# Where 64 rows of the gate and up weights land in SBUF: partitions 32 to 95 in place of 0 to 63 and 64 to 127

## The chip, the core and the metric

The kernel runs on one core of a Trainium2 chip. A core has a matrix engine (PE, whose loading of stationary operands is listed apart as PEld), three engines for elementwise work (DVE, ACT, POOL), a queue engine that issues DMAs (SP), 16 DMA engines between the chip's memory (HBM) and the on-chip memory SBUF, and PSUM, into which PE writes. SBUF has 128 partitions; a tile is a block of partitions by columns. Each engine takes its instructions in the order in which they were written for it, and waits on semaphores for what others produce. The metric is the device time of one execution in microseconds.

## The reference

Forward and backward pass of a small decode block, in bfloat16: a layer norm of `x` (2 rows of 576), attention of 32 query heads over a cache of 16 heads of 4096 positions by 128, and beside it a gated bilinear layer with 4608 columns. Its outputs are the result and the gradients of `x`, both caches and all five weight matrices.

```python
xn = _layernorm(x, axis=-1)
out = x + A(xn, k_cache, v_cache, wq, wo) + B(xn, w_gate, w_up, w_down)

def B(x, w_gate, w_up, w_down):
    g = x @ w_gate          # [2, 576] @ [576, 4608]
    u = x @ w_up
    return (g * u) @ w_down
out, vjp = jax.vjp(f, x, k_cache, v_cache, wq, wo, w_gate, w_up, w_down)
grads = vjp(grad_out)
```

The caches are read once and their gradients written once, in blocks of 1 MB: 92.5 MB in and 92.5 MB out in all, weights included.

## The kernel before

All of it is one program with streams of work: loads of the caches (`load_kv`), loads of weights (`load_ws`), 32-by-32 transposes of what was loaded (`turn`, on DVE), softmax (`attend`), its gradient (`dscores`), the outer products that make the cache gradients (`outer`), the projections per group of heads (`group_front`, `group_back`) and the gated layer in nine slices of 512 columns (`mlp`). A planner (`class Order`) runs through these streams before anything is built, with an estimate for each operation and hand-tuned priorities (`PR`, `OFF`), and so fixes the order on every engine. What it decides is fixed in the program; at run time each engine waits only on semaphores. All large DMAs are issued by SP, in one order; an issue waits until the eighth before it has landed.

The gated layer's weights have 576 rows. Rows 0 to 511 of a pair of slices go to a `big` tile, four rows to each of 128 partitions, in rows of 2 KB (1 KB for the last slice, which is alone). Rows 512 to 575, the rest, go to the tile `gu` (L1158): those of the gate matrix to partitions 0 to 63, those of the up matrix to partitions 64 to 127, in the same columns. There are five pairs of these loads, four of 128 KB and one of 64 KB each. The loads of the rest of `wq` (rows 512 to 575, 512-byte rows, two halves of the columns on the two halves of the partitions, L1132) are made in the same manner and are not touched by the change.

Three steps use `gu`:

- In the forward product (`mlp`, L854) the fifth of five accumulating matmuls takes `gu` as moving operand, with a stationary `xs[:, 4]` (the normed `x` on partitions 0 to 63, zero elsewhere) for the gate and `xs[:, 5]` (on partitions 64 to 127) for up. `front` fills both from two small transposes on PE.
- For the gradient of `x`, `mlp` transposes the weights on DVE: the main part into `X`, `gu` into `Xt` (256 columns of 4 bytes, one instruction for gate and up).
- `dxn` (L678 and L683) multiplies these with stationaries: `wm` for the main part and `wt` for the rest. `stationaries` makes `wm` on DVE (L664) and then two halves of `wt` from it on POOL (L671), one for the partitions of gate and one for those of up. The product has 128 columns for the main part and 32 for the rest, and is added to `accx` (160 columns, L944). The query weights use the same function, with `accx` too (L1085). `final_dx` folds `accx` into the gradient with small float32 matmuls (L1486, L1488).

The softmax steps use small tiles (`mx`, `m4`, `mr`, `negb`, `z`, `rz`, `cs`, `cr`), two sets of them, and constants are made through short-lived tiles (`S64`, `mk16`, `foldf`, `xnb`), each with memory of its own.

Of the kernel before, what the change touches and what calls it, by code (L numbers as in the profile page):

```python
# [250 lines left out]
def DVE(cost):  # L251
    return ("op", "DVE", cost)
# [6 lines left out]
def POOL(cost):  # L259
    return ("op", "POOL", cost)  # L260
# [10 lines left out]
def REL(tag, i):  # L271
    return ("rel", tag, i)
# [24 lines left out]
NBIG, NGU, NWW, NBD = 16, 1, 6, 3  # L297
# [56 lines left out]
def kernel(  # L354
# [31 lines left out]
    GH = 2 * G  # L386
# [8 lines left out]
    FS = 512  # L395
# [11 lines left out]
    def tiles(tag, n, shape, dtype=BF16):  # L407
        od.ring(tag, n)
        return [const.tile(list(shape), dtype, name=f"{tag}{i}") for i in range(n)]

    kv_t = X_t = st_t = G_t = tiles("big", NBIG, [P, NCH * Dh])
    od.share("big", CAP)
    Xt_t = tiles("Xt", 1, [P, FS])
    gu_t = tiles("gu", NGU, [P, 2 * FS])
    ww_t = tiles("ww", NWW, [P, WB])
    tl_t = tiles("tl", 2, [P, FS])
    BD_t = tiles("BD", NBD, [P, 16, Dh])
# [21 lines left out]
    ch_t = []  # L439
    for i in range(2):  # L440
        ch_t.append(dict(
            mx=const.tile([P, 1], FP32, name=f"mx{i}"), m4=const.tile([1, 4], FP32, name=f"m4{i}"),
            mr=const.tile([1, P], FP32, name=f"mr{i}"),
            negb=const.tile([P, 1], FP32, name=f"negb{i}"), ex=const.tile([P, P], FP32, name=f"ex{i}"),
            z=const.tile([P, 1], FP32, name=f"z{i}"), rz=const.tile([P, 1], FP32, name=f"rz{i}"),
            pr=const.tile([P, P], BF16, name=f"pr{i}"), cs=const.tile([P, 1], FP32, name=f"cs{i}"),
            cr=const.tile([P, 1], FP32, name=f"cr{i}"), ds=const.tile([P, P], BF16, name=f"ds{i}"),
            sp=const.tile([P, 2 * P], BF16, name=f"sp{i}")))

# [5 lines left out]
    m_t = banks("m", 2, [P, 512])  # L455
# [4 lines left out]
    def pairs(ap):  # L460
        return ap.bitcast(FP32)

    def t32(out, in_):
        nc.vector.transpose(out, in_)  # L464
# [30 lines left out]
    acc = filled("acc", [P, 5, 2], FP32, 0.0)  # L495
    accx = filled("accx", [P, 160], FP32, 0.0)
    xs = filled("xs", [P, 6, 32], BF16, 0.0)
    Wdy = filled("Wdy", [P, 2, 160], BF16, 0.0)
# [14 lines left out]
    Q4 = const.tile([P, 4], FP32, name="Q4")  # L513
    S64 = const.tile([P, 64], FP32, name="S64")
    G4 = const.tile([P, 32, 4], FP32, name="G4")
    mask8 = const.tile([P, 4, 2], FP32, name="mask8")
    mk16 = const.tile([P, 2, 8], FP32, name="mk16")
    mask16 = const.tile([P, 16], BF16, name="mask16")
    fold = const.tile([P, 4, GH], BF16, name="fold")
    foldf = const.tile([P, 4, GH], FP32, name="foldf")  # L520

# [71 lines left out]
    def front():  # L593
# [31 lines left out]
        nc.vector.tensor_copy(xs[64:128, 5, 0:2], tp[64:128, 10:12])  # L625
        yield REL("m", i)
        yield SET(Exn)
# [33 lines left out]
    def stationaries(i, rep, npos, half, costs):  # L661
        Wm, Wt = wm_t[i], wt_t[i]
        yield DVE(costs[0])
        nc.vector.tensor_tensor(  # L664
            view(Wm[:], 0, P, 0, [[8, npos], [2, 4], [1, 2]]), view(rep, 0, P, 0, [[2, npos], [0, 4], [1, 2]]),
            view(mask8[:], 0, P, 0, [[0, npos], [2, 4], [1, 2]]), ALU.mult)
        yield POOL(costs[1])
        for h in range(2):
            off, dims = half(h)
            n = len(dims) > 1 and dims[0][1] or 1  # L670
            nc.gpsimd.tensor_copy(  # L671
                view(Wt[:], 64 * h, 64, 0, [[dims[-1][1], n], [1, dims[-1][1]]]), view(Wm[:], 64 * h, 64, off, dims))

    def dxn(dp, i, X, S, pos, xoff, xstep, Xt, St, toff, tpos):
        Wm, Wt = wm_t[i], wt_t[i]
        for s in range(S):
            for q in range(4):
                nc.tensor.matmul(dp[32 * q:32 * q + 32, 0:P], lhsT=view(Wm[:], 0, P, 8 * pos(q, s), [[1, 32]]),  # L678
                                 rhs=view(X, 0, P, xoff(q, s), [[xstep, 4], [2, 32]]),
                                 start=(s == 0), stop=(s == S - 1))  # L680
        for s in range(St):
            for q in range(4):
                nc.tensor.matmul(dp[32 * q:32 * q + 32, P:160], lhsT=view(Wt[:], 0, P, 8 * tpos(q, s), [[1, 32]]),  # L683
                                 rhs=view(Xt, 0, P, toff(q, s), [[2, 32]]),
                                 start=(s == 0), stop=(s == St - 1))
# [152 lines left out]
    def mlp(i, hh, sl, Lgu, Ld, wd_slot):  # L838
# [4 lines left out]
        f0 = i * FS  # L843
# [93 lines left out]
        dxn(m_t[m], ws, X[:], 8, lambda q, s: q * 8 + s,  # L937
            lambda q, s: (s // 4) * 4 * FS + (2 * q + (s // 2) % 2) * 64 + s % 2, FS,
            Xt[:], 4, lambda q, s: (2 * q + s // 2) * 64 + s % 2, lambda q, s: 4 * q + s)
# [80 lines left out]
    def group_back(g):  # L1020
# [46 lines left out]
        for be in range(4):  # L1067
# [11 lines left out]
        yield PE(0.24, 0.17, kind="c")  # L1079
        dxn(m_t[m], ws, X[:], 4, lambda q, s: q * 4 + s, lambda q, s: (2 * q + s // 2) * 64 + s % 2, FS,  # L1080
            X[:], 2, lambda q, s: 4 * FS + q * 64 + s, lambda q, s: 2 * q + s)
        yield REL("X", x)
        yield REL("wm", ws)
        yield DVE(0.31)
        nc.vector.tensor_add(accx[:], accx[:], m_t[m][:, 0:160])  # L1085
        yield REL("m", m)
# [36 lines left out]
    def load_w(item):  # L1123
# [20 lines left out]
        else:  # L1144
# [6 lines left out]
            for w, Wsrc in enumerate((B_w_gate, B_w_up)):  # L1151
                b = yield ACQ("G")
                sl["G"].append(b)
                yield DMA("SP", 0.4, 128 * 4 * width * 2, 2 * width)
                nc.sync.dma_start(G_t[b][:, 0:4 * width].rearrange("p (c n) -> p c n", n=width),
                                  Wsrc[0:512, f0:f0 + width].rearrange("(p c) n -> p c n", c=4))
                yield DMA("SP", 0.36, 64 * width * 2, 2 * width)
                nc.sync.dma_start(gu[64 * w:64 * w + 64, 0:width], Wsrc[512:576, f0:f0 + width])  # L1158
            yield ("lset", Lgu)
# [317 lines left out]
    def final_dx():  # L1477
# [7 lines left out]
        yield PE(0.3, 0.3)  # L1485
        nc.tensor.matmul(mt[:, 0:8], lhsT=accx[:, 0:P], rhs=F8[:], start=True, stop=True)  # L1486
        for k in range(2):
            nc.tensor.matmul(mt[0:32, 8:12], lhsT=accx[:, P:160], rhs=F8[:, 4 * k:4 * k + 4],  # L1488
                             start=(k == 0), stop=(k == 1))
        rows_add(o, 1)  # L1490
# [69 lines left out]
```

## Time and profile before

| | |
|---|---|
| device time, three runs | 477.23, 479.78, 479.92 us; median 479.78 |
| profiled execution: span from the first to the last instruction | 475.9 us |
| profiled execution's own time | the page gives none beside the span; the three runs are 1.3 to 4.0 us above it |
| bytes | 92.48 MB read, 92.48 MB written; 389 GB/s over the span |
| mean granted clock of PE | 0.713 |
| DMA packets | 41925 |
| `gu` loads, issue to landing (min / median / max) | 10.1 / 12.6 / 14.6 us |

The profile is of one execution. Its page lists the busy time of each engine, the DMA queues, the chain of work that ended last (followed back from the last instruction to what released it, again and again), and the costliest groups of instructions by line: engine, operation, output and inputs, shapes, count, then busy time in us and the mean of one in ns, then the idle time of the engine ahead of them and what ended it. A table by stretches gives the busy time of each engine between two times, with the DMA share (the mean busy share of the 16 engines) and the rate in GB/s. Busy time of an engine that is not on the chain costs nothing.

### The profile page before, as it was taken

The numbers are of one execution on the slowest core, as the hardware profiler recorded it, in microseconds if no ns is written. First come the engines' busy times: TensorE is split into PE (matmuls) and PEld (weight loads), VectorE is DVE, ScalarE is ACT, GpSimd is POOL, SyncE is SP. The second block draws the span as 40 slices with busy tenths as digits, with TensorE's granted clock in tenths as the row PEclk, the third lists the DMA queues.
The fourth block names the chain that finished last, engine by engine and source line by source line (L and its number), as shares of the span: only waits on it lengthen the run. The fifth ranks groups of instructions, "written<-read, shape, count | busy, mean of one in ns | idle before, by whom it ended". The sixth has DMA issues, their size and how long they took to land.

```text
span 475.9 us, 15396 instructions
## 1 busy us (share of the span) xinstructions
PE 369.1 (78%) x6546; PEld 214.3 (45%) x6546; DVE 369.3 (78%) x708; ACT 335.2 (70%) x507; POOL 152.4 (32%) x208
## 2 busy tenths in 40 slices
PE   1588589879598868678768977797777879878894
PEld 1455344445464535454453444563334424434463
DVE  8897878869658976687758868899577958888771
ACT  3149569958676886536779764599676987898971
POOL 0440154351004443004634510051644656333000
PEclk9979585758756678577767685679665866776965
DMA  8999999999999999999999999999999999999994
GB/s 317 364 401 420 399 410 402 355 392 423 419 400 390 391 356 420 424 407 375 370 407 372 324 412 421 419 412 398 337 425 417 416 416 421 423 420 392 425 354 185
DMA packets 41925, 185.95 MB, mean 391 GB/s; under 512 B 3960, under 2 KB 13440, under 8 KB 25472
## 3 DMA queue, kind: packets, MB, share of 16 engines
q1 hardware_dynamic: 41848, 184.96, 98.4%
q8 instruction: 51, 0.84, 0.7%
q14 instruction: 18, 0.15, 0.1%
q10 hardware_dynamic: 8, 0.00, 0.0%
HBM read 92.48 MB, written 92.48 MB: 389 GB/s over the span
## 4 chain that ended last, share of the span: by engine, by line
DMA 46%; PE 21%; DVE 15%; ACT 10%; issue 4%; POOL 2%; SPq 1%; DVEq 0%; ACTq 0%; POOLq 0%
DMA out_dram<-big 20%; DMA big<-in_A_v_cache_dram 12%; DVE big L464 10%; ACT big L468 8%; DMA big<-in_A_k_cache_dram 8%; PE ps_o L1255 4%; PE ps_m L1234 4%; DMA ww<-in_A_wo_dram 3%; PE ps_o L722 3%; DMA gu<-in_B_w_up_dram 3%; DVE big L470 2%; PE ps_m L1407 2%; POOL BD L1222 2%; PE ps_m L678 1%; PE ps_o L759 1%
## 5 line engine op out<-in xcount | busy, mean ns | idle before, releaser
L468 ACT CAST big<-ps_o 128x1024 bf16<-128x1024 f32 (+2 forms) x310 | 277.4, 960 | 45.7 <-PE ps_o L1255 20.0
L464 DVE STREAM_TRANSPOSE big<-big 128x1024 f32<-128x1024 f32 x146 | 175.9, 1224 | 28.8 <-DMA out_dram<-big 16.8
L1222 POOL TENSOR_TENSOR BD<-vr,mask 128x2048 bf16<-128x2048 bf16 x32 | 115.3, 3604 | 102.6 <-ACT vr L468 48.6
L470 DVE CAST big<-ps_o 128x1024 bf16<-128x1024 f32 (+2 forms) x68 | 74.4, 1095 | 15.8 <-PE ps_o L722 5.2
L1234 PE MATMUL ps_m<-big,W 128*32 128x128 bf16 x2048 | 59.1, 279 | 10.2 <-ACT Q L468 3.4
L1234 PEld LDWEIGHTS <-W 128*32 128x32 bf16 x2048 | 46.1, 123 | 27.1 <-issue 25.2
L671 POOL COPY wt<-wm 64x128 bf16<-64x128 bf16 (+1 forms) x34 | 8.9, 263 | 139.5 <-DVE wm L664 119.3
L1255 PE MATMUL ps_o<-BD,dd 32*128 32x512 bf16 x256 | 45.3, 476 | 10.2 <-ACT big L468 8.0
L1255 PE MATMUL ps_o<-BD,pp 32*128 32x512 bf16 x256 | 47.1, 507 | 6.2 <-ACT big L468 3.5
L1199 POOL COPY W<-rep 32x16 bf16<-32x16 bf16 x128 | 24.9, 194 | 54.1 <-DVE rep L983 32.2
L464 DVE STREAM_TRANSPOSE big<-ww 128x1152 f32<-128x1152 f32 x25 | 34.0, 1361 | 6.9 <-DMA ww<-in_A_wo_dram 3.5
L1407 PE MATMUL ps_m<-big,pp 128*32 128x512 bf16 x256 | 27.9, 507 | 5.0 <-DMA big<-in_A_v_cache_dram 4.3
L1255 PEld LDWEIGHTS <-dd 32*128 32x128 bf16 x256 | 12.2, 98 | 32.3 <-issue 26.9
L1407 PE MATMUL ps_m<-big,dd 128*32 128x512 bf16 x256 | 24.7, 473 | 0.8 <-DVE acc L919 0.6
L1255 PEld LDWEIGHTS <-pp 32*128 32x128 bf16 x256 | 10.4, 96 | 27.1 <-issue 23.6
L759 PEld LDWEIGHTS <-xnr 32*128 32x128 bf16 x368 | 12.9, 114 | 12.3 <-issue 10.9
L722 PE MATMUL ps_o<-dyr,R 32*32 32x288 bf16 x256 | 17.1, 398 | 1.7 <-ACT big L468 1.3
L872 PE MATMUL ps_m<-big,Wdy 128*128 128x128 bf16 x162 | 15.0, 265 | 2.9 <-DVE rz L1320 1.4
L722 PE MATMUL ps_o<-dyr,hb 32*32 32x288 bf16 x288 | 16.2, 346 | 0.4 <-ACT big L468 0.2
L759 PE MATMUL ps_o<-D,xnr 32*128 32x128 bf16 x256 | 13.3, 281 | 3.4 <-ACT big L468 1.5
L872 PEld LDWEIGHTS <-Wdy 128*128 128x128 bf16 x162 | 13.4, 119 | 5.0 <-issue 5.0
L678 PE MATMUL ps_m<-big,wm 128*32 128x128 bf16 x416 | 12.7, 280 | 3.4 <-DVE rz L1320 1.2
(205 smaller groups left out, 478.2 us busy)
## 6 DMA issues: line engine op xcount, KB each, us to landing
out_dram<-big SPq DMA_DIRECT2D x74, 1024.0 KB, 12.6
big<-in_A_k_cache_dram SPq DMA_DIRECT2D x32, 1024.0 KB, 13.8
big<-in_A_v_cache_dram SPq DMA_DIRECT2D x32, 1024.0 KB, 13.5
out_dram<-big SPq DMA_DIRECT2D x17, 576.0 KB, 11.0
ww<-in_B_w_down_dram SPq DMA_DIRECT2D x9, 576.0 KB, 12.8
ww<-in_A_wo_dram SPq DMA_DIRECT2D x8, 576.0 KB, 7.3
ww<-in_A_wq_dram SPq DMA_DIRECT2D x8, 512.0 KB, 8.1
big<-in_B_w_gate_dram SPq DMA_DIRECT2D x4, 1024.0 KB, 11.5
```

Source lines behind the costliest of these rows:

```text
L464: nc.vector.transpose(out, in_)
L468: nc.scalar.copy(out, in_)
L470: nc.vector.tensor_copy(out=out, in_=in_)
L678: nc.tensor.matmul(dp[32 * q:32 * q + 32, 0:P], lhsT=view(Wm[:], 0, P, 8 * pos(q, s), [[1, 32]]), rhs=view(X, 0, P, xoff(q, s), [[xstep, 4 ...
L722: nc.tensor.matmul(o[32 * q:32 * q + 32, aa, 0:HD2], lhsT=view(t, 32 * q, 32, 2 * A + aa, [[4, 32]]), rhs=dyr[32 * q:32 * q + 32, k * HD2: ...
L759: nc.tensor.matmul(o[:, aa, j * P:(j + 1) * P], lhsT=xnr[32 * a:32 * a + 32, dc * P:(dc + 1) * P], rhs=rhs(a), start=True, stop=True)
L872: nc.tensor.matmul(dh, lhsT=Wdy[:, e, 2 * k:2 * k + P], rhs=view(X[:], 0, P, 64 * k + e, [[D, FC], [2, 32]]), start=(k == 0 and e == 0), s ...
L1199: nc.gpsimd.tensor_copy(view(W_t[t][w][:], 32 * a, 32, 6 + 8 * a, [[G * WW, 4], [WW, G], [1, 2]]), view(rep_t[grp[g]["qs"]][:], 32 * a, 32 ...
L1222: nc.gpsimd.tensor_tensor(BD_t[i][:], view(vr_t[v][:], 0, P, 0, [[0, 16], [1, Dh]]), view(mask16[:], 0, P, 0, [[1, 16], [0, Dh]]), ALU.mult)
L1234: nc.tensor.matmul(sc[32 * cq:32 * cq + 32, :], lhsT=view(W[:], 0, P, (be * G + l) * WW + 6 - 4 * c2 - 2 * l, [[1, 32]]), rhs=view(X[:], 0 ...
L1255: nc.tensor.matmul(o[:, k, :], lhsT=pr2[32 * c4:32 * c4 + 32, :], rhs=BD[32 * c4:32 * c4 + 32, 8 * l + 4 * h2:8 * l + 4 * h2 + 4, :], star ...
L1407: nc.tensor.matmul(ct[32 * j:32 * j + 32, :], lhsT=view(rT, 0, P, 4 * c + 2 * l, [[1, 32]]), rhs=kv_t[kvS[s][t][l]][:, Dh * c:Dh * (c + 4) ...
```

## The change

The rest of both matrices now goes to partitions 32 to 95, in columns of their own: gate in the first half of the columns of `gu`, up in the second, so that `gu` is twice as wide. Partitions 0 to 31 and 96 to 127 of it are cleared once, by two instructions on POOL, since PE multiplies all 128 partitions. What follows from it:

- one stationary `xs[:, 6]` (the normed `x` on partitions 32 to 95) in place of two; `front` makes it with one more transpose on PE and two copies on DVE. `xs[:, 4]` and `xs[:, 5]` stay for the query weights;
- `Xt` has twice the columns, and its transpose takes 512 columns of 4 bytes in place of 256;
- in `dxn`, `mlp` uses `wm` itself for the rest, with 32 matmuls in place of 16 for each slice; the two copies to `wt` on POOL are left out for the nine slices (18 instructions). Those for the query weights stay;
- the rest's product of the slices goes to columns 0 to 31 of `accx`, that of the query weights to 160 to 191, so that `accx` has 192 columns and `final_dx` a third small product;
- to make room, the small tiles of a softmax set become columns of one tile `small`, `mr` lies in the tile `sp`, `S64`, `mk16` and `foldf` in `ex` of the first set, and `xnb` in the last `BD` tile.

Apart from what is added and left out, the instructions stand in the same order on every engine, the DMAs on SP's queue too. In the waits, the copy to `sp` waits for ACT in one place more, the first transpose of `gu` also waits for POOL (the clearing), and some of DVE's `wm` products no longer wait for POOL.

```diff
-    Xt_t = tiles("Xt", 1, [P, FS])
-    gu_t = tiles("gu", NGU, [P, 2 * FS])
+    Xt_t = tiles("Xt", 1, [P, 2 * FS])
+    gu_t = tiles("gu", NGU, [P, 4 * FS])
...
+        small = const.tile([P, 12], FP32, name=f"small{i}")
         ch_t.append(dict(
...
+            {k: small[:, j:j + 1] for j, k in enumerate(("mx", "negb", "z", "rz", "cs", "cr"))}, m4=small[0:1, 8:12],
+            ex=const.tile([P, P], FP32, name=f"ex{i}"), pr=const.tile([P, P], BF16, name=f"pr{i}"),
+            ds=const.tile([P, P], BF16, name=f"ds{i}"), sp=const.tile([P, 2 * P], BF16, name=f"sp{i}")))
+        ch_t[i]["mr"] = ch_t[i]["sp"][0:1].bitcast(FP32)
...
-    accx = filled("accx", [P, 160], FP32, 0.0)
-    xs = filled("xs", [P, 6, 32], BF16, 0.0)
+    accx = filled("accx", [P, 192], FP32, 0.0)
+    xs = filled("xs", [P, 7, 32], BF16, 0.0)
+    for t in gu_t:
+        for r in (slice(0, 32), slice(96, P)):
+            nc.gpsimd.memset(t[r], 0.0)
...
-    S64 = const.tile([P, 64], FP32, name="S64")
+    S64 = ch_t[0]["ex"][:, 0:64]
...
-    xnb = const.tile([2, D], BF16, name="xnb")
+    xnb = BD_t[NBD - 1][0:2].rearrange("p a d -> p (a d)")[:, 0:D]
...
+        nc.tensor.transpose(tp[0:96, 12:14], xnb[:, 480:576], ident[0:2, 0:2])
...
+        for r in (slice(32, 64), slice(64, 96)):
+            nc.vector.tensor_copy(xs[r, 6, 0:2], tp[r, 12:14])
...
         yield POOL(costs[1])
+        if half is None:
+            return
...
-                t, c0 = (main[w], width * dc + FS * hh) if dc < 4 else (gu, FS * hh)
+                t, c0 = (main[w], width * dc + FS * hh) if dc < 4 else (gu, 2 * FS * w + FS * hh)
...
-                    nc.tensor.matmul(ug[32 * a:32 * a + 32, 1 - w, :], lhsT=xs[:, dc if dc < 4 else 4 + w, :],
+                    nc.tensor.matmul(ug[32 * a:32 * a + 32, 1 - w, :], lhsT=xs[:, dc if dc < 4 else 6, :],
...
-        yield from stationaries(ws, rp, 32, lambda h: (32 * h, [[64, 4], [1, 32]]), (0.42, 0.6))
+        yield from stationaries(ws, rp, 32, None, (0.42, 0.6))
...
-        t32(pairs(Xt[:]), pairs(gu[:, FS * hh:FS * (hh + 1)]))
+        t32(pairs(Xt[:]).rearrange("p (w n) -> p w n", w=2),
+            pairs(gu[:]).rearrange("p (w n) -> p w n", w=2)[:, :, HFS * hh:HFS * (hh + 1)])
...
-            Xt[:], 4, lambda q, s: (2 * q + s // 2) * 64 + s % 2, lambda q, s: 4 * q + s)
+            wm_t[ws], Xt[:], 8, lambda q, s: q * 8 + s,
+            lambda q, s: (s // 4) * FS + (2 * q + (s // 2) % 2) * 64 + s % 2, 0)
...
-        nc.vector.tensor_add(accx[:], accx[:], m_t[m][:, 0:160])
+        nc.vector.tensor_add(accx[:, 0:160], accx[:, 0:160], m_t[m][:, 0:160])
...
-                nc.sync.dma_start(gu[64 * w:64 * w + 64, 0:width], Wsrc[512:576, f0:f0 + width])
+                nc.sync.dma_start(gu[32:96, 2 * FS * w:2 * FS * w + width], Wsrc[512:576, f0:f0 + width])
...
-        nc.tensor.matmul(mt[:, 0:8], lhsT=accx[:, 0:P], rhs=F8[:], start=True, stop=True)
-        for k in range(2):
-            nc.tensor.matmul(mt[0:32, 8:12], lhsT=accx[:, P:160], rhs=F8[:, 4 * k:4 * k + 4],
-                             start=(k == 0), stop=(k == 1))
+        nc.tensor.matmul(mt[:, 0:8], lhsT=accx[:, 32:160], rhs=F8[:], start=True, stop=True)
+        for k, (c, j) in enumerate(((160, 0), (160, 4), (0, 2))):
+            nc.tensor.matmul(mt[0:32, 8:12], lhsT=accx[:, c:c + 32], rhs=F8[:, j:j + 4],
+                             start=(k == 0), stop=(k == 2))
```

More of the change, by code (lines that the diff above doesn't have):

```diff
@@ L425 @@
     wm_t = tiles("wm", 2, [P, 35, 8])
-    wt_t = [const.tile([P, 19, 8], BF16, name=f"wt{i}") for i in range(2)]
+    wt_t = [const.tile([P, 11, 8], BF16, name=f"wt{i}") for i in range(2)]
     oT_t = tiles("oT", 2, [P, 2, GH, 32])
@@ L440 @@
     for i in range(2):
+        small = const.tile([P, 12], FP32, name=f"small{i}")
         ch_t.append(dict(
[L442 to L448, printed above, removed]
+            {k: small[:, j:j + 1] for j, k in enumerate(("mx", "negb", "z", "rz", "cs", "cr"))}, m4=small[0:1, 8:12],
+            ex=const.tile([P, P], FP32, name=f"ex{i}"), pr=const.tile([P, P], BF16, name=f"pr{i}"),
+            ds=const.tile([P, P], BF16, name=f"ds{i}"), sp=const.tile([P, 2 * P], BF16, name=f"sp{i}")))
+        ch_t[i]["mr"] = ch_t[i]["sp"][0:1].bitcast(FP32)
     def banks(tag, n, shape):
@@ L513 @@
     Q4 = const.tile([P, 4], FP32, name="Q4")
-    S64 = const.tile([P, 64], FP32, name="S64")
+    S64 = ch_t[0]["ex"][:, 0:64]
     G4 = const.tile([P, 32, 4], FP32, name="G4")
     mask8 = const.tile([P, 4, 2], FP32, name="mask8")
-    mk16 = const.tile([P, 2, 8], FP32, name="mk16")
+    mk16 = ch_t[0]["ex"][:, 64:80].rearrange("p (l c) -> p l c", l=2)
     mask16 = const.tile([P, 16], BF16, name="mask16")
     fold = const.tile([P, 4, GH], BF16, name="fold")
-    foldf = const.tile([P, 4, GH], FP32, name="foldf")
+    foldf = ch_t[0]["ex"][:, 80:80 + 4 * GH].rearrange("p (w r) -> p w r", w=4)
     Exn, Exr, Edy, Econst, Ezero = Event(), Event(), Event(), Event(), Event()
@@ L672, in stationaries, with dxn @@
                 view(Wt[:], 64 * h, 64, 0, [[dims[-1][1], n], [1, dims[-1][1]]]), view(Wm[:], 64 * h, 64, off, dims))
-    def dxn(dp, i, X, S, pos, xoff, xstep, Xt, St, toff, tpos):
-        Wm, Wt = wm_t[i], wt_t[i]
+    def dxn(dp, Wm, X, S, pos, xoff, xstep, Wt, Xt, St, tpos, toff, t0):
         for s in range(S):
             for q in range(4):
-                nc.tensor.matmul(dp[32 * q:32 * q + 32, 0:P], lhsT=view(Wm[:], 0, P, 8 * pos(q, s), [[1, 32]]),
+                nc.tensor.matmul(dp[32 * q:32 * q + 32, 32:160], lhsT=view(Wm[:], 0, P, 8 * pos(q, s), [[1, 32]]),
                                  rhs=view(X, 0, P, xoff(q, s), [[xstep, 4], [2, 32]]),
@@ L682, in dxn @@
             for q in range(4):
-                nc.tensor.matmul(dp[32 * q:32 * q + 32, P:160], lhsT=view(Wt[:], 0, P, 8 * tpos(q, s), [[1, 32]]),
+                nc.tensor.matmul(dp[32 * q:32 * q + 32, t0:t0 + 32], lhsT=view(Wt[:], 0, P, 8 * tpos(q, s), [[1, 32]]),
                                  rhs=view(Xt, 0, P, toff(q, s), [[2, 32]]),
@@ L936, in mlp @@
         yield PE(0.48, 0.34, kind="c")
-        dxn(m_t[m], ws, X[:], 8, lambda q, s: q * 8 + s,
+        dxn(m_t[m], wm_t[ws], X[:], 8, lambda q, s: q * 8 + s,
             lambda q, s: (s // 4) * 4 * FS + (2 * q + (s // 2) % 2) * 64 + s % 2, FS,
-            Xt[:], 4, lambda q, s: (2 * q + s // 2) * 64 + s % 2, lambda q, s: 4 * q + s)
+            wm_t[ws], Xt[:], 8, lambda q, s: q * 8 + s,
+            lambda q, s: (s // 4) * FS + (2 * q + (s // 2) % 2) * 64 + s % 2, 0)
         yield REL("X", x)
@@ L1079, in group_back @@
         yield PE(0.24, 0.17, kind="c")
-        dxn(m_t[m], ws, X[:], 4, lambda q, s: q * 4 + s, lambda q, s: (2 * q + s // 2) * 64 + s % 2, FS,
-            X[:], 2, lambda q, s: 4 * FS + q * 64 + s, lambda q, s: 2 * q + s)
+        dxn(m_t[m], wm_t[ws], X[:], 4, lambda q, s: q * 4 + s, lambda q, s: (2 * q + s // 2) * 64 + s % 2, FS,
+            wt_t[ws], X[:], 2, lambda q, s: 2 * q + s, lambda q, s: 4 * FS + q * 64 + s, 160)
         yield REL("X", x)
@@ L1084, in group_back @@
         yield DVE(0.31)
-        nc.vector.tensor_add(accx[:], accx[:], m_t[m][:, 0:160])
+        nc.vector.tensor_add(accx[:, 32:192], accx[:, 32:192], m_t[m][:, 32:192])
         yield REL("m", m)
```

## The prediction, made before the changed kernel was run

> **What bounds the kernel now.** First the page: busy shares, the main DMA queue, the chain of waits by engine.
>
> ```profile
> PE 369.1 (78%) x6546; PEld 214.3 (45%) x6546; DVE 369.3 (78%) x708; ACT 335.2 (70%) x507; POOL 152.4 (32%) x208
> q1 hardware_dynamic: 41848, 184.96, 98.4%
> DMA 46%; PE 21%; DVE 15%; ACT 10%; issue 4%; POOL 2%; SPq 1%; DVEq 0%; ACTq 0%; POOLq 0%
> ```
>
> No engine is above 78%, while packets fill 98.4% of the 16 DMA engines' time and the chain is nearly half DMA. So bytes per second count first. The second view is the table by stretch: start and end in us, length, busy time of PE, PEld, DVE, ACT and POOL, granted clock, DMA share (packets overlap a little, so it can pass 1), GB/s.
>
> ```profile
> core 0: us, PE busy (x) PEld busy (x) DVE busy (x) ACT busy (x) POOL busy (x), PEclk, DMA share, GB/s
> 11.50:13.50 2.00, 0.54 (x5) 0.37 (x5) 1.97 (x4) 0.68 (x2) 0.00 (x0) 1.00 1.05 388
> 13.50:15.50 2.00, 0.68 (x20) 0.59 (x19) 1.97 (x7) 0.00 (x0) 0.68 (x4) 1.00 1.06 259
> 17.00:19.50 2.50, 2.15 (x42) 1.78 (x30) 2.47 (x4) 0.31 (x1) 2.46 (x3) 1.00 1.06 320
> 90.00:91.50 1.50, 1.47 (x38) 0.83 (x37) 1.48 (x2) 0.90 (x1) 0.41 (x1) 0.56 1.04 407
> 91.50:93.50 2.00, 2.00 (x41) 0.96 (x35) 1.71 (x5) 1.91 (x3) 0.00 (x0) 0.50 1.07 268
> 93.50:95.50 2.00, 1.34 (x7) 0.50 (x7) 2.00 (x3) 1.78 (x4) 0.00 (x0) 0.98 1.05 345
> 95.50:98.50 3.00, 2.34 (x20) 0.54 (x19) 1.54 (x4) 3.00 (x6) 1.55 (x8) 0.75 1.06 306
> 102.00:120.00 18.00, 16.79 (x329) 10.45 (x329) 15.23 (x29) 12.63 (x20) 5.65 (x4) 0.76 1.01 423
> 167.50:170.00 2.50, 2.10 (x43) 1.13 (x45) 2.05 (x5) 2.50 (x5) 1.43 (x3) 0.73 1.03 402
> 170.00:172.00 2.00, 2.00 (x45) 0.99 (x44) 2.00 (x5) 1.31 (x3) 2.00 (x1) 0.50 1.09 295
> 175.50:178.00 2.50, 0.62 (x25) 0.62 (x28) 1.93 (x4) 2.17 (x3) 0.00 (x0) 0.50 1.08 306
> 267.00:269.50 2.50, 2.50 (x67) 1.66 (x67) 2.25 (x4) 2.19 (x4) 0.08 (x1) 0.50 1.07 322
> 269.50:271.50 2.00, 2.00 (x33) 0.55 (x25) 2.00 (x6) 0.00 (x0) 2.00 (x1) 0.61 1.06 344
> 271.50:274.00 2.50, 2.13 (x34) 1.60 (x30) 2.50 (x5) 2.41 (x6) 2.24 (x5) 1.00 1.08 267
> 428.00:431.00 3.00, 2.31 (x66) 1.31 (x55) 3.00 (x7) 1.58 (x3) 0.00 (x0) 0.99 1.02 386
> 434.00:437.00 3.00, 2.72 (x12) 1.02 (x9) 2.31 (x4) 2.51 (x4) 2.59 (x1) 0.50 1.04 351
> ```
>
> The stretch at 102 us is the rate with 8 KB rows, 423 GB/s. Gate and up weights come in rows of 2 KB at 388 to 407. In ten short stretches the rate falls to 259 to 345 while the engines stay full (share 1.05 to 1.09): the packets get slower. What else happens there is told by the tile `gu` (issue times, and time from issue to landing) in the first 40 us:
>
> ```profile
> L1158 SPq DMA_DIRECT2D gu<-in_B_w_gate_dram x1: 505/505/505, 5.7 to 5.7; - x1
> L1158 SPq DMA_DIRECT2D gu<-in_B_w_up_dram x1: 1893/1893/1893, 6.9 to 6.9; - x1
> DMA to landing us min/median/max: 10.7/11.9/13.2
> ```
>
> The gate load of `gu` lands at 5.7 + 10.7 = 16.4, the up load at 6.9 + 13.2 = 20.1: each just after a dip. The other dips lie likewise behind the other `gu` loads. The large 128-partition loads beside them have the same 2 KB rows and run at 388 and more, so I put the dips on what the change moves: 64 rows written to half of the partitions.
>
> **The change part by part.** *The loads.* I take 400 GB/s as the rate without dips, between the 2 KB rows' 388 to 407 and the 423 of 8 KB rows. A dip loses length × (1 − rate/400): 0.70 + 0.50 for the first pair of loads; 0.66 + 0.28 + 0.70 for the second; 0.53 + 0.59 for the third; 0.49 + 0.28 + 0.83 for the fourth: 5.56 us. The last pair has 1 KB rows: 3 × (1 − 351/386) = 0.27. Together **5.8 us** (5.3 against 388, 6.6 against 420). No load onto partitions 32 to 95 is in this trace: the saving lies between 0 (the dips stay) and 6.6. I take 5.8, because the nearest rows, loads over both halves of the partitions, show no dip.
>
> [...]
>
> *How much reaches the end.* Rows of the chain (start, length):
>
> ```profile
> 10.06 15.12 DMA big<-in_A_v_cache_dram
> 99.18 17.30 DMA out_dram<-big
> 166.00 13.84 DMA gu<-in_B_w_up_dram
> 271.60 14.94 DMA out_dram<-big
> ```
>
> The first, third and fourth contain dips. The second starts behind the dips of 91.5 to 98.5, but a transfer of 1 MB at 423 GB/s takes 2.5 us, so most of its 17.3 is backlog, and that is shorter by what was saved before. Against it stand places where the DMA ran dry and computing set the pace:
>
> ```profile
> 224.00:226.00 2.00, 1.82 (x28) 0.56 (x21) 1.97 (x4) 2.00 (x4) 1.21 (x7) 1.00 0.73 223
> 255.00:258.00 3.00, 2.31 (x33) 1.22 (x31) 3.00 (x5) 3.00 (x4) 1.36 (x7) 0.90 0.61 254
> 461.00:464.00 3.00, 3.00 (x67) 2.25 (x68) 1.31 (x3) 1.63 (x3) 0.00 (x0) 0.50 0.59 215
> ```
>
> There 2 × 0.27 + 3 × 0.39 + 3 × 0.41 = 2.9 us are idle. Computing that starts from an earlier landing moves along; what is late for other reasons doesn't. I take 0.8 of the saving as reaching the end, **4.6 us**; the bounds are 0.3 and 1.
>
> *The added work.* Rows by form, and from the listing in order of time:
>
> ```profile
> 464.31 0.32 PE L683 MATMUL ps_m<-Xt,wt 128*32 128x32 bf16 x16
> 465.63 0.38 PE L1488 MATMUL ps_m<-F,accx 128*32 128x4 f32 x4
> L464 DVE STREAM_TRANSPOSE Xt<-gu 128x256 f32<-128x256 f32 x9 | 3.8, 421 | 0.0
> L464 DVE STREAM_TRANSPOSE big<-big 128x1024 f32<-128x1024 f32 x146 | 175.9, 1224 | 28.8 <-DMA out_dram<-big 16.8
> L671 POOL COPY wt<-wm 64x128 bf16<-64x128 bf16 x18 | 5.2, 289 | 65.5 <-DVE wm L664 65.1
> ```
>
> Each of nine slices gets 32 instead of 16 small matmuls: + 0.32 us, 2.9 in all. Its transpose of `Xt` goes from 256 to 512 columns: at (1224 − 421)/768 = 1.05 ns a column + 0.27 us, 2.4 in all. By the chain's shares 21% of the former and 15% of the latter lie on the path: 0.6 + 0.4 = 1.0 us; the rest is hidden behind queued transfers. If it were not, it would be 5.3. At the end nothing hides: + 0.32 for the last slice and + 0.19 for the third small product of `final_dx` (two passes more of four taking 0.38): 0.5. Both together **1.5 us**.
>
> 18 copies on POOL go, 5.2 us of it, and the 65 us in which POOL stood in order behind them. I count nothing: in the view of the tile `wt` PE never waits for them, since they ran beside DVE's transposes of `X`, which PE needs as well; and what POOL does next still waits for its own inputs. If the path ran through them, up to 5.2 would be gained.
>
> ```profile
> 0.73 0.20 POOL masks.py:197 MEMSET ident<- 128x128 bf16 x1 [0.29 <-POOLq L1544]
> 14.70 0.93 POOL L1199 COPY W<-rep 32x16 bf16<-32x16 bf16 x4 [13.38 <-DVE nmu L637]
> 22.71 1.38 DVE L464 STREAM_TRANSPOSE big<-ww 128x1152 f32<-128x1152 f32 x1 [1.04 <-DMA ww<-in_B_w_down_dram]
> 25.20 2.37 DVE L464 STREAM_TRANSPOSE big<-big 128x1024 f32<-128x1024 f32 x2 [0.97 <-DMA big<-in_A_v_cache_dram]
> 10.64 0.16 DVE L625 COPY xs<-ps_m 64x2 bf16<-64x2 bf16 x1
> ```
>
> The two clears of `gu` on POOL have 2048 columns: at 0.20 us for 128 columns up to 3.2 us each, 6.4 together, inside 13.38 us in which POOL idles, and over before the first gate load has landed at 16.4; SP's queue waits for neither. If they held DVE up by as much, it would take 6.4, of which the waits for DMA at 22.7 and 25.2 absorb 2.0; no row shows such a hold-up, so 0. Two more copies to `xs` add 2 × 0.16 us, before the V load lands at 25.2, and hide there. The tiles that share memory take turns on one chain of softmax steps; instructions and waits keep their order on each engine, SP's included. I price that at 0; the range takes in 0.5 for it.
>
> **The sum.** 475.9 us of span − 4.6 + 1.5 = 472.8, or − 3.1. The runs shown are 1.3 to 4.0 us above the span; from their median 479.78 comes **476.7 us**.
>
> **The rivals.** *All of it arrives:* the bursts go, and the added matmuls and transposes hide except for the last 0.5: 479.8 − 5.8 + 0.5 = 474.5. For it speaks that the DMA was dry for so little of the time; against it, the 54% of the chain that isn't DMA.
>
> *The change doesn't do what it says:* the dips belong to the source, 64 short rows of a wide matrix, and not to the partitions. Then the loads stay as slow and the added work remains: 479.8 + 1.5 = 481.3. For it: both kinds of load read with the same pitch, and no row tells the source from the target. Against it: 402 GB/s on the same matrix right before the dip at 170. [...]
>
> *Slower:* the dips stay and PE and DVE can't hide the slices' extra work, because both take their work in a fixed order and every attention step behind a slice waits for it. The price is all of 2.9 + 2.4 plus 0.2 at the end: 479.8 + 5.5 = 485.3. It decides if over nine tenths of the 5.3 lie on the path, where the chain's shares say a fifth.
>
> **How the numbers follow.** The forecast (475 to 479) has 0.45, all of it arriving 0.27, the unchanged dips 0.20, slower 0.08. One per cent, 4.8 us, is about what a measurement here tells from no change. Faster by more: 0.27; within: 0.65; slower by more: 0.08. The range goes from 473.0 (474.5, less 1.5 for the scatter of the runs and a saving of 6.6) to 481.8 (481.3 + 0.5 for the shared tiles).
>
> **What would show it.** Right: behind each pair of `gu` loads the stretches read 380 GB/s and more, and the queue's share of 16 engines' time falls by about 5.8 us; `Xt` transposes take about 0.69 us, the 32 matmuls about 0.64. The step on the path is wrong if the rates rise and the span stays: then the stretches with idle DMA have grown by as much. The forecast is wrong altogether if the rates of 259 to 345 are still there.

## The result, and the profile after

The changed kernel takes **474.26 us** (median of 4 runs, 473.63 to 474.44) beside 478.66 for the kernel before on the same chip: a ratio of 0.9909, 95% interval 0.9883 to 0.9934. A second comparison, on another occasion, gave 473.38 us (472.84 to 473.75) beside 478.94: 0.9889, 0.9872 to 0.9906. So the change saves 4.4 and 5.6 us, about 1%; the forecast was 3.1 us and 476.7.

The first rows of the page of the kernel after (busy time and share of the span by engine; the main DMA queue with packets, MB and share of 16 engines; the chain of waits by engine):

```profile
PE 378.8 (80%) x6693; PEld 218.3 (46%) x6693; DVE 373.6 (79%) x710; ACT 335.1 (71%) x507; POOL 150.8 (32%) x192
q1 hardware_dynamic: 41848, 184.96, 98.2%
DMA 39%; PE 31%; DVE 12%; ACT 11%; issue 3%; SPq 1%; POOL 1%; DVEq 0%; ACTq 0%; POOLq 0%
```

The same 184.96 MB go through the queue, still 98% full. The page heads a span of 472.5 us, so the packets fill 0.982 × 472.5 = 464.0 us where they filled 0.984 × 475.9 = 468.3: 4.3 us less. In a second profile of the kernel after (98.3% of 471.6 us) it is 463.6, 4.7 less. The forecast had 5.8. DMA's share of the chain falls from 46 to 39%, PE's rises from 21 to 31% (40 and 27% in the second profile).

The table by stretch of the kernel after (columns as in the prediction: start and end, length, busy PE, PEld, DVE, ACT and POOL, granted clock, DMA share, GB/s). The first six rows are the places behind the five pairs of `gu` loads, the last five are those where the DMA runs dry:

```profile
12.00:21.00 9.00, 5.54 (x118) 4.79 (x115) 8.85 (x19) 0.78 (x3) 4.72 (x7) 1.00 1.05 405
94.00:98.00 4.00, 3.15 (x43) 1.46 (x42) 3.64 (x6) 3.78 (x5) 0.00 (x0) 0.78 1.06 396
170.00:174.00 4.00, 4.00 (x84) 2.05 (x82) 3.29 (x6) 3.07 (x5) 3.92 (x3) 0.50 1.02 410
175.00:180.00 5.00, 2.73 (x60) 1.75 (x58) 3.72 (x6) 3.98 (x5) 0.00 (x0) 0.77 1.05 407
268.00:273.00 5.00, 4.56 (x65) 2.23 (x54) 5.00 (x9) 2.93 (x6) 4.20 (x5) 0.82 1.06 403
434.00:438.00 4.00, 3.89 (x84) 2.01 (x76) 2.86 (x6) 3.33 (x6) 1.14 (x1) 0.61 1.03 426
...
50.00:54.00 4.00, 1.35 (x5) 0.62 (x6) 4.00 (x7) 0.91 (x3) 0.00 (x0) 0.67 0.90 310
69.00:71.00 2.00, 1.80 (x80) 1.30 (x72) 1.40 (x3) 1.90 (x3) 2.00 (x1) 1.00 0.71 295
222.00:224.00 2.00, 1.69 (x12) 0.72 (x9) 0.65 (x4) 1.80 (x3) 0.00 (x0) 0.50 0.90 356
255.00:257.00 2.00, 1.16 (x7) 0.38 (x6) 2.00 (x5) 2.00 (x3) 0.03 (x1) 0.79 0.80 332
458.00:460.00 2.00, 2.00 (x48) 1.25 (x49) 0.68 (x2) 1.26 (x3) 0.00 (x0) 0.50 0.46 166
```

The dips of 259 to 345 GB/s are gone: the same places run at 396 to 426. The stretches that were dry before are no worse: 0.2 + 0.4 + 1.1 = 1.7 us are idle where it was 2.9. But two further ones have come, 4 × 0.10 + 2 × 0.29 = 1.0 us. They show where this execution lost something again, in the 50 us behind the first pair. Here is that stretch in the kernel before, the kernel after, and the second profile of the kernel after, one fence each:

```profile
40.00:90.00 50.00, 39.18 (x749) 22.33 (x749) 39.08 (x76) 38.87 (x59) 18.45 (x25) 0.73 1.01 403
```

```profile
40.00:90.00 50.00, 41.21 (x769) 23.69 (x769) 38.05 (x74) 37.24 (x56) 15.44 (x23) 0.65 0.99 376
```

```profile
40.00:90.00 50.00, 39.60 (x805) 23.30 (x809) 40.49 (x80) 39.73 (x60) 18.27 (x23) 0.74 1.00 396
...
69.00:71.00 2.00, 1.28 (x19) 0.66 (x20) 0.87 (x6) 1.05 (x2) 0.81 (x2) 1.00 1.03 426
```

At 376 instead of 403 GB/s this execution moved 50 × 27 = 1.35 MB less in the stretch, 3.3 us at 405 GB/s; it cannot be all the change's, for the same kernel's second profile moved 396 there, and was not dry at 69 us. A part of it may be. Six other runs with the kernel after's products and fast loads (e3, e5 and e7 to e10 below) moved 383 to 403 in this stretch, while the two without the added work moved 401 and 402; no run settles it. A single execution's span is therefore good to some 2 or 3 us only, and the verdicts below go by medians and ratios.

### The profile page after: what moved, and what is told of

The parts are those of the page before. It is cut to its first block, busy times and chain, and to the rows that moved or that the text cites. A ratio compares the mean times of both kernels' runs of the same rounds, so it can differ in the third digit from the quotient of the medians.

```text
span 472.5 us, 15670 instructions
## 1 busy us (share of the span) xinstructions
PE 378.8 (80%) x6693; PEld 218.3 (46%) x6693; DVE 373.6 (79%) x710; ACT 335.1 (71%) x507; POOL 150.8 (32%) x192
## 3 DMA queue, kind: packets, MB, share of 16 engines
q1 hardware_dynamic: 41848, 184.96, 98.2%
## 4 chain that ended last, share of the span: by engine, by line
DMA 39%; PE 31%; DVE 12%; ACT 11%; issue 3%; SPq 1%; POOL 1%; DVEq 0%; ACTq 0%; POOLq 0%
DMA out_dram<-big 15%; DMA big<-in_A_v_cache_dram 13%; ACT big L466 9%; DMA big<-in_A_k_cache_dram 8%; DVE big L462 7%; PE ps_o L1262 6%; PE ps_m L1241 6%; PE ps_m L1414 3%; PE ps_o L727 3%; DMA ww<-in_A_wo_dram 2%; DVE big L468 2%; PE ps_m L683 2%; PE ps_o L764 1%; PE ps_m L1006 1%; PE ps_m L1325 1%
## 5 line engine op out<-in xcount | busy, mean ns | idle before, releaser
L1262 PE MATMUL ps_o<-BD,dd 32*128 32x512 bf16 x256 | 46.4, 485 | 11.2 <-ACT big L466 8.5
L1262 PE MATMUL ps_o<-BD,pp 32*128 32x512 bf16 x256 | 48.4, 522 | 6.0 <-ACT big L466 4.0
L677 POOL COPY wt<-wm 64x64 bf16<-64x64 bf16 x16 | 3.7, 232 | 101.8 <-DVE wm L668 70.7
L1414 PE MATMUL ps_m<-big,pp 128*32 128x512 bf16 x256 | 29.0, 527 | 3.7 <-DMA big<-in_A_v_cache_dram 3.1
L727 PE MATMUL ps_o<-dyr,hb 32*32 32x288 bf16 x288 | 17.4, 367 | 0.4 <-ACT big L466 0.2
L877 PE MATMUL ps_m<-big,Wdy 128*128 128x128 bf16 x162 | 15.3, 268 | 1.3 <-DVE acc L924 0.7
L1006 PE MATMUL ps_m<-big,Wdy 128*128 128x128 bf16 x144 | 14.9, 284 | 0.4 <-DVE small L1366 0.2
```

Of the source, the lines that this page charges most:

```text
L727: nc.tensor.matmul(o[32 * q:32 * q + 32, aa, 0:HD2], lhsT=view(t, 32 * q, 32, 2 * A + aa, [[4, 32]]), rhs=dyr[32 * q:32 * q + 32, k * HD2: ...
L877: nc.tensor.matmul(dh, lhsT=Wdy[:, e, 2 * k:2 * k + P], rhs=view(X[:], 0, P, 64 * k + e, [[D, FC], [2, 32]]), start=(k == 0 and e == 0), s ...
L1006: nc.tensor.matmul(dp, lhsT=Wdy[:, e, 2 * k:2 * k + P], rhs=view(X[:], 0, P, 64 * k + e, [[D, GH], [2, 32]]), start=(k == 0 and e == 0), s ...
L1262: nc.tensor.matmul(o[:, k, :], lhsT=pr2[32 * c4:32 * c4 + 32, :], rhs=BD[32 * c4:32 * c4 + 32, 8 * l + 4 * h2:8 * l + 4 * h2 + 4, :], star ...
L1414: nc.tensor.matmul(ct[32 * j:32 * j + 32, :], lhsT=view(rT, 0, P, 4 * c + 2 * l, [[1, 32]]), rhs=kv_t[kvS[s][t][l]][:, Dh * c:Dh * (c + 4) ...
```

## The experiments

All ratios are to the kernel before on the same chip. "Pair-one rate" is the row of the table by stretch from 12 to 21 us, in which the first two `gu` loads land and all kernels still lie alike in time. Times and rates:

| run | us, median | ratio, 95% interval | pair-one rate, GB/s |
|---|---|---|---|
| before | 477.8 to 478.94 | 1 | 344 |
| after | 474.26 | 0.9909 (0.9883 to 0.9934) | 405 |
| after, again | 473.38 | 0.9889 (0.9872 to 0.9906) | 406 |
| e1, half the partitions | 479.70 | 1.0033 (1.0011 to 1.0055) | 315 |
| e2, no doubled work | 472.88 | 0.9880 (0.9846 to 0.9914) | 408 |
| e2, again | 472.60 | 0.9882 (0.9861 to 0.9902) | 408 |
| e3, POOL copies back | 473.17 | 0.9880 (0.9847 to 0.9913) | 409 |
| e4, quarters | 476.83 | 0.9966 (0.9947 to 0.9985) | 364 |
| e5, short clears | 473.34 | 0.9897 (0.9873 to 0.9920) | 406 |
| e6, odd and even rows | 476.73 | 0.9957 (0.9938 to 0.9976) | 368 |
| e7, every second partition | 473.35 | 0.9896 (0.9868 to 0.9923) | 403 |
| e8, half rows | 473.31 | 0.9900 (0.9871 to 0.9930) | 404 |
| e9, 32 rows spread | 473.18 | 0.9878 (0.9825 to 0.9931) | 408 |
| e10, source step | 472.72 | 0.9888 (0.9842 to 0.9933) | 410 |

The kernel before's own row, for comparison:

```profile
12.00:21.00 9.00, 5.92 (x149) 4.94 (x148) 8.02 (x20) 1.50 (x5) 5.13 (x9) 1.00 1.05 344
```

### The placing alone, undone (e1)

```diff
-            nc.sync.dma_start(gu[32:96, 2 * FS * w:2 * FS * w + width], Wsrc[512:576, f0:f0 + width])
+            nc.sync.dma_start(gu[0:64, 2 * FS * w:2 * FS * w + width], Wsrc[512:576, f0:f0 + width])
```

The clears, the copies to `xs` and the columns in `final_dx` move with it.

> The kernel after with one thing undone: both gu loads of a pair go to partitions 0 to 63, at the same addresses, times and sizes. The added matmuls and transposes stay, the 18 copies on POOL stay away, the tiles that share memory stay. Theory (the dips come from 64 rows on one half of the partitions, and the kernel gains by their absence): behind the gu loads the stretches of 2 to 3 us fall to 260 to 345 GB/s again, and the time is about 478.5 us, 477 to 480, some 4 above the kernel after. Since both loads of a pair now go to the same half, the dips may be a little deeper than before. Rival (the gain comes from POOL's missing copies or from the shared tiles): the dips come back or not, and the time stays within 0.7 of 474.3.

Measured: 479.70 us, 1.0033 of the kernel before. The rival falls. Its table by stretch, at the first and the fourth pair:

```profile
12.00:21.00 9.00, 5.68 (x122) 4.90 (x119) 8.84 (x19) 0.68 (x2) 4.62 (x7) 1.00 1.05 315
...
273.00:275.00 2.00, 1.91 (x24) 1.04 (x17) 1.78 (x4) 1.60 (x3) 1.92 (x4) 0.59 1.08 288
```

The dips are back. In the first pair they are deeper than in the kernel before, where the two loads of a pair go to different halves (315 against 344); in the fourth they are not (288 here, 267 in the prediction's table). With the source, the sizes, the order and all other work the kernel after's, the placing alone is worth 1.0033 − 0.9889 = 1.4% by the one comparison and 1.0033 − 0.9909 = 1.2% by the other, 5.9 to 6.9 us, each with an uncertainty of about 1.5.

### The added work, taken away (e2, twice)

```diff
-        t32(pairs(Xt[:]).rearrange("p (w n) -> p w n", w=2),
-            pairs(gu[:]).rearrange("p (w n) -> p w n", w=2)[:, :, HFS * hh:HFS * (hh + 1)])
+        t32(pairs(Xt[:, 0:FS]), pairs(gu[:, FS * hh:FS * (hh + 1)]))
...
-            wm_t[ws], Xt[:], 8, lambda q, s: q * 8 + s,
+            wm_t[ws], Xt[:], 4, lambda q, s: q * 8 + s,
```

> The kernel after without the added work per slice: the transpose of Xt takes 256 columns instead of 512 and 16 small matmuls follow instead of 32. That leaves the up matrix's rows 512 to 575 out of the gradient of x. It measures what the added 2.9 us of PE and 2.5 us of DVE cost. The prediction's share (1.0 on the path and 0.3 at the end): 1.3 below the kernel after, about 473.0. Rival, all hidden but the last slice's: 0.3 below, 474.0. Rival, all of it on the path: 5.4 below, 468.9.

> The kernel after without the added work per slice once more (256 columns in the transpose of Xt, 16 small matmuls; the up matrix's rows 512 to 575 are left out of the gradient of x), now beside the kernel after on the same chip. By the prediction's share 1.3 below it; if only the last slice's work counts 0.3; if all of it counts 5.4. The first run, 0.988 of the kernel before, lies at 1.4 below with an uncertainty of about 2.

Measured: 472.88, then 472.60 us, the latter 0.8 below the kernel after's 473.38 beside it. The table by stretch for the tile `Xt` alone (PE busy, then DVE, over the whole span), first of the kernel after, then of this run:

```profile
0.00:476.00 476.00, 3.97 (x288) 6.19 (x9) 0.70 0.98 391
```

```profile
0.00:476.00 476.00, 2.78 (x144) 3.80 (x9) 0.71 0.98 391
```

The last slice's matmuls in the listing in order of time (start, length), in the same order:

```profile
460.68 0.45 PE L688 MATMUL ps_m<-Xt,wm 128*32 128x32 bf16 x32
```

```profile
460.05 0.32 PE L688 MATMUL ps_m<-Xt,wm 128*32 128x32 bf16 x16
```

So the change adds 6.19 − 3.80 = 2.4 us on DVE, and 3.97 − 2.78 = 1.2 us on PE. All of it on the path is excluded: that would be 5.4 by the expectation, 3.6 by these rows. The ratios differ by 0.0007 with an uncertainty of 0.0027, that is 0.3 ± 1.3 us, so the 1.3 expected isn't excluded, nor is nothing. The first run gives a second reading: e1 has the dips of the kernel before and the added work, and is 0.33% (0.11 to 0.55) slower, 1.6 us (0.5 to 2.6). What the added work costs is therefore known only as something between nothing and 2.6 us.

Against the kernel before, this run shows what the faster loads are worth without the added work: 478.94 − 472.60 = 6.3 us by the medians, 5.7 by the ratio, and 5.7 both ways in the first comparison.

### POOL's copies, put back (e3)

```diff
-        yield from stationaries(ws, rp, 32, None, (0.42, 0.6))
+        yield from stationaries(ws, rp, 32, lambda h: (32 * h, [[64, 2], [1, 32]]), (0.42, 0.6))
```

> The kernel after with two copies of 64 partitions per slice put back on POOL, from wm into wt, at the place where the kernel before has them; nothing reads them, so PE does not wait for them, but POOL does them in its fixed order. Theory (their removal gave nothing): within 0.5 of the kernel after, 474.3. Rival (a part of the gain came from POOL's order): up to 5.2 above the kernel after if each copy were on the path, 475.5 or more if a quarter of it is.

Measured: 473.17 us, 0.9880; the kernel after has 0.9909 and 0.9889. The view of the tile `wt` (with the copies that the attention's slices keep; duration min/median/max) shows that they were done, 18 more than the 16 of the kernel after. They move 64 columns each, where those of the kernel before move 128, and take 232 ns in place of 289:

```profile
L677 POOL COPY wt<-wm x34: 228/232/235, 32.9 to 454.6; 64x64 bf16<-64x64 bf16 x34
  DVE wm L668: 116.7, 16
```

POOL waits behind them again, 116.7 us for `wm` where it is 70.7 in the kernel after, and no cost is seen. The rival, 475.5 or more, lies above all its runs (471.31 to 473.78).

### Quarters (e4)

```diff
-                nc.sync.dma_start(gu[32:96, 2 * FS * w:2 * FS * w + width], Wsrc[512:576, f0:f0 + width])
+                for k in range(2):
+                    p0 = 64 * k + 32 * w
+                    nc.sync.dma_start(gu[p0:p0 + 32, 0:width], Wsrc[512 + 32 * k:544 + 32 * k, f0:f0 + width])
```

The tiles `Xt` and `gu` are as narrow as in the kernel before, and four copies of 32 partitions per slice put the gate's and up's coefficients into `wt`.

> Another placing that touches both halves and needs no doubled work: each gu load is two DMAs of 32 rows, the gate's onto partitions 0 to 31 and 64 to 95, the up's onto 32 to 63 and 96 to 127, so that one 256-column transpose and 16 matmuls serve both; four copies of 32 partitions on POOL per slice (the kernel before has two of 64); no clears of gu. Theory A (what counts is that a pair of DMAs that are in flight together reaches both halves): the dips stay away, and the saved work brings it to 472 to 474. Theory B (each DMA of 32 rows lies in one half and is written at that half's rate): the dips are back behind the loads, and the time is 477 to 479.

Measured: 476.83 us, 0.9966. Theory B: although a pair's DMAs are in flight together and reach both halves, the dips are there, if less deep than before:

```profile
12.00:21.00 9.00, 5.67 (x116) 4.76 (x119) 8.47 (x20) 1.13 (x3) 5.12 (x9) 1.00 1.06 364
```

In the first pair that is 364 GB/s, against 405 where one DMA reaches both halves.

### The clears of gu, shortened (e5)

```diff
-            nc.gpsimd.memset(t[r], 0.0)
+            nc.gpsimd.memset(t[r].bitcast(FP32), 0.0)
```

> The kernel after with the same two clears of gu on POOL written as 1024 columns of fp32 instead of 2048 of bf16. In the kernel after they run from 1.26 to 5.45 us and a copy on DVE (G from K) that begins at 4.16 takes 1.38 us instead of 0.23, so DVE is 1.0 us late. If a column costs the same in either type, the clears end at about 3.4 and the copy takes 0.23 again. The prediction priced the hold-up at 0: then the time is that of the kernel after. Rival (with the dips gone, DVE is what the first down weights and V wait for, so the lost microsecond is still there): 0.7 to 1.3 below the kernel after.

Measured: 473.34 us, beside 473.38 of the kernel after. From the listing in order of time, the kernel after and this run:

```profile
1.26 4.19 POOL L498 MEMSET gu<- 32x2048 bf16 x2
3.50 0.21 DVE L530 CAST identf<-ident 128x128 f32<-128x128 bf16 x1
4.16 1.38 DVE L537 COPY G<-K 128x128 f32<-128x128 f32 x1
```

```profile
1.26 1.94 POOL L498 MEMSET gu<- 32x1024 f32 x2
4.30 0.23 DVE L537 COPY G<-K 128x128 f32<-128x128 f32 x1
```

The hold-up was there, 1.15 us for one copy, until POOL was done at 5.45; it goes with the shorter clears (which end at 3.20), and the time stays. The prediction's price of nothing is right; its reason, that no row shows such a hold-up, is not.

### Odd and even rows, and four runs that take it apart (e6 to e10)

If one DMA has to reach both halves, cutting each load into odd and even rows, 32 in each DMA, should do no harm.

```diff
-                nc.sync.dma_start(gu[32:96, 2 * FS * w:2 * FS * w + width], Wsrc[512:576, f0:f0 + width])
+                for k in range(2):
+                    nc.sync.dma_start(gu[32 + k:96:2, 2 * FS * w:2 * FS * w + width],
+                                      Wsrc[512 + k:576:2, f0:f0 + width])
```

> The kernel after with each gu load cut into two DMAs of 32 rows, like the run with quarters, but the even rows onto the even and the odd rows onto the odd partitions of 32 to 95: the same bytes at the same places, the same number of DMAs as with quarters, and each of them reaches both halves. Theory (what counts is whether one DMA's rows lie in one half): the 2 KB packets are fast again and the time is within 1 us of the kernel after, 473 to 474.5. Rival (short DMAs of 32 rows are slow by themselves): dips as with quarters, 476 to 477.5.

Measured: 476.73 us, 0.9957. The theory falls, and the rival's number holds:

```profile
12.00:21.00 9.00, 5.61 (x118) 4.79 (x115) 8.85 (x19) 0.70 (x3) 4.72 (x7) 1.00 1.06 368
```

So 368 GB/s, against 405 with all 64 rows in one DMA: reaching both halves in one DMA is not enough by itself. Four more runs take it apart:

```diff
e7
+                nc.sync.dma_start(gu[0:P:2, 2 * FS * w:2 * FS * w + width], Wsrc[512:576, f0:f0 + width])
e8
+                for k in range(2):
+                    c = width // 2 * k
+                    nc.sync.dma_start(gu[32:96, 2 * FS * w + c:2 * FS * w + c + width // 2],
+                                      Wsrc[512:576, f0 + c:f0 + c + width // 2])
e9
+                for k in range(2):
+                    nc.sync.dma_start(gu[2 * k:P:4, 2 * FS * w:2 * FS * w + width],
+                                      Wsrc[512 + 32 * k:544 + 32 * k, f0:f0 + width])
e10
+                nc.sync.dma_start(gu[32:96, 2 * FS * w:2 * FS * w + width], Wsrc[448:576:2, f0:f0 + width])
```

> The kernel after with each gu load, still one DMA of 64 rows, on every second partition from 0 to 126 instead of on 32 to 95; the whole of gu is cleared once at the start. The products with features 512 to 575 then take the wrong rows, so what these features give to the output and the gradients is not the reference's; number, size and order of all instructions are the kernel after's. The run with odd and even rows left it open what matters. Theory C (a DMA of 64 rows must reach both halves evenly): no dips, 473 to 474. [...]

> The kernel after with each gu load cut into two DMAs of 64 rows by half the columns (rows of 1 KB instead of 2 KB, at the same places): as many DMAs as in the runs with quarters and with odd and even rows, but each with 64 rows on 32 to 95. If in those two runs the number of rows per DMA made the dips, there are none here, and the time is within 1 us of the kernel after, 473 to 474.5. Rival (each further small DMA among the large ones makes a dip, whatever its rows): dips and 476 to 477.5.

> The kernel with every second partition once more, but each gu load cut into two DMAs of 32 rows: rows 512 to 543 onto partitions 0, 4, 8 and so on to 124, rows 544 to 575 onto 2, 6 and so on to 126. As there, the products with features 512 to 575 take the wrong rows; instructions are the same but for the added DMAs. Each DMA is spread evenly over both halves, and its source rows lie one behind the other. The run with half rows has shown that the number of DMAs makes no dips. If 32 rows in one DMA make them, they are here: 476 to 477.5. If the dips of the run with odd and even rows came from its source's step of two rows or from its order of partitions, there are none here: 473 to 474.5.

> The kernel after with the source of each gu load changed alone: every second row from 448 to 574 of the gate and up weights instead of rows 512 to 575, still 64 rows in one DMA onto partitions 32 to 95. The products with features 512 to 575 then use other weights' rows, so what these features give is not the reference's; instructions, sizes and order are the kernel after's. If the step in the source made the dips of the run with odd and even rows, they are here: 476 to 477.5. If the 32 rows per DMA made them, there are none: 473 to 474.5.

Measured: 473.35, 473.31, 473.18 and 472.72 us, and no dip in any. The row of the one with every second partition, then that of the 32 rows spread over all:

```profile
12.00:21.00 9.00, 6.05 (x128) 5.07 (x131) 8.36 (x20) 1.13 (x4) 5.11 (x9) 1.00 1.05 403
```

```profile
12.00:21.00 9.00, 5.32 (x107) 4.56 (x106) 7.97 (x18) 0.70 (x3) 4.71 (x7) 1.00 1.06 408
```

Theory C holds for these: rows spread evenly over both halves are as good as rows on 32 to 95, in DMAs of 64 or of 32 rows. Neither the number of DMAs (half rows), nor 32 rows in one (32 rows spread), nor a step of two rows in the source (source step) makes a dip alone, so the rival to the odd and even rows was right in its number only. With 32 rows spread, the quarters have their reason: the same two DMAs of 32 rows run at 408 GB/s over both halves and at 364 in one. What made the dips of the odd and even rows **stays open**: left are the step of two rows in the source together with 32 rows in a DMA, and the placing on every second partition from 32 to 95.

### The kernel after, again

> The kernel after itself, unchanged, beside the next three on one chip. Its first measurement gave 0.9909 of the kernel before (0.9883 to 0.9934), the one with the two copies back on POOL 0.9880 (0.9847 to 0.9913). If that difference is only the scatter of the runs, the kernel after falls between 472.5 and 474.5 us here, and single runs between 471 and 475. If the copies on POOL did help, it stays at 474 or above.

Measured: 473.38 us; single runs from 472.84 to 473.75. So its first 0.9909 and the 0.9880 with the copies back differ by no more than the scatter of the runs.

## Why the prediction was right, and where not

**The dips and their cause** (5.8 us): right. The placing alone brings them back (e1), and without the added work their absence is worth 5.7 us. A check from rows of the first pair: nine microseconds at 344 instead of 405 GB/s are 9 × (1 − 344/405) = 1.36 us, times four pairs (the fifth has short rows) 5.4. The same sum gives 8.0 for e1 (measured against the kernel after: 5.9 to 6.9), 3.6 for the quarters (against e2: 0.9966 − 0.9881, 4.1) and 3.3 for the odd and even rows (against the kernel after: 0.9957 − 0.9889, 3.3). The first pair stands for all four here, and for e1, where it is the deepest, that is too much.

The packets in the traces give the sum without that assumption. Added up by size over the whole run, as a share of 16 engines, the packets of 2 KB (the gate and up weights) take 28.7 us in the kernel before and 25.0 in the kernel after. Those of 4608 bytes, which belong to `wo`, `w_down` and their gradients and to no `gu` load, take 53.6 and 51.3. So 6.1 us go, and 2.4 of them from transfers that the change doesn't touch: the loads on half of the partitions slowed what was in flight beside them. Above the kernel after, these two sizes take 6.4 us more in e1, 4.0 in the quarters and 3.7 in the odd and even rows.

**How much reaches the end** (0.8, so 4.6 us): this step failed; about all of it does, 5.7 of 5.8 by e2, with an interval of 4.7 to 6.7 by its second comparison and 4.1 to 7.4 by its first, so that the 4.6 lies at the edge. The runs with dips agree: 6.4, 4.0 and 3.7 us of packets cost 5.9 to 6.9, 4.1 and 3.3. The prediction looked for the loss in dry stretches behind the savings. Those that were there shrank from 2.9 to 1.7 us; the new ones at 50 and 69 us, 1.0 us, are in one execution and mostly not in the next. The first rival, that all of it arrives, had the better term, and its 474.5 us is the nearest of the numbers given: 474.26 and 473.38 were measured. The forecast's own band, 475 to 479 us at 0.45, missed both; what came is the case that had 0.27.

**The added work** (1.5 us): not settled: 0.8 by the medians and 0.3 ± 1.3 by the ratios of e2, 1.6 (0.5 to 2.6) by e1. DVE's term was sized rightly (6.19/9 = 0.69 us a transpose, as forecast), PE's was not: 32 matmuls in a row take 0.45 us, not 0.64; the second 16 add only 0.13. At the end, 0.5 was forecast; there the last slice adds 0.13. Six passes of the small product take 0.35 us in the kernel after, where four took 0.38, but the granted clock was 1.00 there and 0.50 in the kernel before. In e2's second run, also at 0.50, six take 0.48, which is 0.10 more than four. The kernel after, then that run:

```profile
461.90 0.35 PE L1495 MATMUL ps_m<-F,accx 128*32 128x4 f32 x6
```

```profile
461.36 0.48 PE L1494 MATMUL ps_m<-F,accx 128*32 128x4 f32 x6
```

So the end gets about 0.2 us longer at the same clock, not 0.5.

**POOL's copies** at nothing: right (e3). The reason given holds too: POOL waits for its next inputs instead. The group of its multiplications into `BD` (busy time, mean ns | idle before, what ended most of it) on the page of the kernel before, then after:

```profile
L1222 POOL TENSOR_TENSOR BD<-vr,mask 128x2048 bf16<-128x2048 bf16 x32 | 115.3, 3604 | 102.6 <-ACT vr L468 48.6
```

```profile
L1229 POOL TENSOR_TENSOR BD<-vr,mask 128x2048 bf16<-128x2048 bf16 x32 | 115.3, 3603 | 140.9 <-DVE vr L468 73.2
```

The idle time ahead of it grows by 38 us.

**The clears** at nothing, with a bound of 6.4: right in the sum, wrong in the mechanism (e5). DVE was held up for 1.15 us, in the copy of `G` (1.38 us, 0.23 with the short clears). A cast at 3.50 us, within the clears as well, took 0.21.

**The two copies to `xs`, the shared tiles** at nothing: nothing here speaks against it; neither was tried alone.

**The sum** came out low by 1.3 to 2.5 us of saving: 1.1 from the share; whether the rest is the added work or the size of the dips, the runs don't separate. The time, 476.7, was off by a further microsecond, as the median it started from, 479.78 of three runs, was high: later medians of the kernel before are 477.8 to 478.94. The range, 473.0 to 481.8, held the time, near its lower end. Of the rivals, "the dips belong to the source" fell with e1, and "slower" with it, as the dips are gone and the work hides.

## What to carry to other kernels

Where a queue is full throughout, look for short stretches with full engines and few GB/s, and ask which load lands just behind them: here a 128 KB load on half of the partitions slowed other packets in flight too and cost over 1 us per pair. Spread such a load over both halves within one DMA, and look at the rate afterwards, since one such placing (odd and even rows) kept its dips. Pay for it with work on engines that wait for the DMA anyway: 2.4 us on DVE and 1.2 on PE bought 5.7. Where a queue is the bound and the saving lies in the queue, it can arrive nearly in full, as 5.7 of 6.1 us did here.

## What the runs showed of the hardware that was not expected

- 64 rows need not lie side by side to be fast: every second partition of 128 (403 GB/s) is as good as 32 to 95 (405), and so are 32 rows in steps of four (408). But 32 rows in steps of two from 32 on are not (368), and none of the runs says why.
- Both loads of a pair on one half cost no more over the whole run than one on each: the packets of 2 KB and 4608 bytes take 82.6 us against 82.3, though the first pair is slower (315 against 344 GB/s).
- More than a third of the loss lies in packets of other transfers: 2.4 of 6.1 us.
- Two clears of 32 partitions on POOL took 4.19 us with 2048 columns in bf16 and 1.94 with 1024 in fp32, the same bytes: here the time went by columns. While the longer ones ran, a copy on DVE that began at 4.16 us took 1.38 in place of 0.23, and a cast that began at 3.50 took 0.21.
